# Two 256-token runs joined for their last eight steps, the first stage re-ordered, and scores put beside the v_m w_in blocks

## The chip, the cores and the metric

One Trainium2 chip, one of its cores. The metric is device time in microseconds (us) of one execution. The kernel before was timed three times: 733.68, 734.61 and 735.14 us, median 734.61.

## The reference

Eight batches, eight heads, 576 tokens, head size 64, 32 memory slots. All inputs are float32.

```python
a    = softmax(phi, axis=tokens)                 # (b, h, s, 32)
k_m  = einsum('bhsm,bhsd->bhmd', a, k)           # 32 memories per head
v_m  = einsum('bhsm,bhsd->bhmd', a, v)
attn = softmax(q @ k_m^T / 8, axis=-1)           # (b, h, s, 32)
x    = (attn @ v_m) with the heads side by side  # 4608 tokens x 512
out  = relu(x @ w_in)**2 @ w_out                 # 512 -> 2048 -> 512
```

## The kernel before

**Algebra.** The kernel never forms x. Since x @ w_in = attn @ (v_m w_in), it makes for each batch a product u = v_m w_in (256 rows, one per head and memory slot, by 2048 columns, in four blocks of 512 columns) and multiplies the attention weights a (256 rows by tokens) by it. Operands of the large products are split into a high and a low fp32r part, so a product is three matmuls: hi·hi, lo·hi, hi·lo.

**Steps.** A batch's tokens are cut into a run of 320 (WIDE) and one of 256 (NARROW). A step is one run with one of 16 tiles f of 128 hidden columns. `ffn1` (L583 to L624) does 6 matmuls (three products by two groups of heads) per piece into a PSUM tile `h`; ScalarE takes the relu (L602), VectorE the square (L608), and ScalarE and GpSimd split it into `g_hi`, `g_lo` (L618, L619). `ffn2` (L628) adds the tile's share to four PSUM accumulators `acc`: 12 matmuls (four tiles of outputs by three products). In the first 16 steps w_out tiles 0 to 3 aren't split yet and 4 plain fp32 matmuls are used (L633), each of which is two instructions. `ffn2` runs two steps behind `ffn1` (LEAD, L733). From batch 2 on, batches come in pairs: 16 steps of 320, 16 joined steps of 512 (256 tokens of each batch; 12 `ffn1` matmuls of 256, 12 `ffn2` matmuls of 512), and 16 steps of 320. Batches 0 and 1 have 64 steps of 320 or 256, in the twelve runs of L740; where a run stops before tile 16, `close` (L659) puts the sums aside in SBUF and adds later ones to them.

**Side work.** Each step has two half steps (L1013): `half(2k)` is called after `ffn1` of step k, `half(2k+1)` after `ffn2` of step k-2. The lists `plan` (L853), `early` and `late` (L948, L971) say by hand at which half each part of a side task is issued; a task is a generator, and each number in its tuple is where its next part goes. Each engine runs its instructions in this order, and so does SyncE's DMA queue (SP). Places in `early` and `late` count from the first half of a pair of batches (`begin`, L986), and those of `early` are negative: they lie in the pair before.

- `task_attend` (L357): scores (`by_heads`, L347: 8 products on 64x32 pieces of the array, 16 instructions, L353) into the PSUM tile `ps_m`; two VectorE transposes (L373), maximum, subtraction, exponential, sum, product, transpose back, and the split into `a_hi`, `a_lo`.
- `task_u` (L726, `make_u` L468): one block of u: `by_heads` over 512 columns into `ps_m`, a ScalarE copy `u_hi` (L478), a VectorE subtraction `u_lo` (L480). There is one `ps_m` (two banks), so attend and u take turns. `h` (pool `ps_h`) has two buffers, one bank each.
- `task_exp`, `task_mem`: softmax of phi and the memories of a batch (L283: 80 matmuls of 128x32 pieces).
- `decode_in`, `decode_out` (L491): the weights arrive as 64-bit words and are put back into floats by two ScalarE and three VectorE instructions and an addition (L518) on VectorE or GpSimd, whichever the place names. Split w_out then takes a ScalarE copy (L575) and a VectorE subtraction (L577).
- `spin` (L143): matmuls of an identity matrix with no use for the result.
- `task_stream`: a 1 MB block of decoded w_in back from device memory into the one tile `w0`, from batch 2 on.

The opening (L826 to L844) is a list of its own, `order`, over phi's softmax (e), batch 0's memories (m), four decodes (d0 to d3), the first two attends (a0, a1) and half a u block (u0). The DMAs ahead of it are in `loads` (L792).

Of the kernel before, what the change touches and what calls it, by code (L numbers as in the profile page):

```python
# [8 lines left out]
F32 = mybir.dt.float32  # L9
F32R = mybir.dt.float32r  # L10
# [14 lines left out]
def attn_moe_kernel(ctx: ExitStack, tc: tile.TileContext, qT, kv, phi, w_in, w_out, outT):  # L25
# [331 lines left out]
    def attend(b, t, q, mem, new_a):  # L357
# [14 lines left out]
        for half in range(2):  # L372
            nc.vector.transpose(flat[:, half * T:(half + 1) * T], sc[half][:, :T])  # L373
        done_ps(ps)
# [5 lines left out]
        yield  # L380
        nc.vector.tensor_tensor(out=st, in0=st, in1=mx[:, :, None].broadcast_to(st.shape), op=ALU.subtract)
# [344 lines left out]
    def task_u(b, n, n0=0, n1=FC):  # L726
        got = state[b]["u"].setdefault(n, [])
        w = w_at.pop((b, n)) if (b, n) in w_at else w_in_at[n]
        if (b, n) not in streamed:
            assert all(("in", 2 * n + i, qd) in ready for i in range(n0 // HC, n1 // HC) for qd in range(NQ))  # L730
        return make_u(b, n, state[b]["mem"], (n0, n1, w), got)

    LEAD = 2  # L733
# [7 lines left out]
        (((i // NT, i % NT),), Q4 * k0, Q4 * k1) for i, k0, k1 in (  # L741
            (0, 0, 1), (1, 0, 1), (2, 0, 1), (3, 0, 2), (2, 1, 2), (1, 1, 2), (0, 1, 3),
            (3, 2, 3), (0, 3, 4), (3, 3, 4), (1, 2, 4), (2, 2, 4),
        )
    ]
    for b in range(2, B, 2):
# [42 lines left out]
    def next_kv():  # L789
# [3 lines left out]
        (first_phi,),  # L793
        (first_kv, 0),
        (first_kv, 1),
        (task_q, 0, 0),
        (fetch_w_in, 0, 0),
# [22 lines left out]
    for fn, *args in loads[:later]:  # L820
# [11 lines left out]
        "d3": lambda: decode_in(1, 1),  # L832
# [6 lines left out]
        "e e e e e d0 m m m m a0 d1 d2 a1 d0 a0 a0 d1 d0 a0 a0 d3 d1 u0 d3 a0 a0 u0 u0 d3 d2 d2"  # L839
# [8 lines left out]
    for n in kept:  # L848
# [5 lines left out]
        ((2,), lambda: spin(1, ident, ps_acc.tile([P, 512], F32, name="acc0"))),  # L854
        ((0, 1, 2), decode_out, 0, nc.vector, True),
        ((0, 1, 1), decode_out, 1, nc.gpsimd, True),
        ((2, 2, 2), task_u, 0, 0, HC, 2 * HC),
        ((3,), lambda: spin(5, ident, ps_acc.tile([P, 512], F32, name="acc3"))),
        ((0,), fetch_w_in, 5, 1),
        ((0,), task_q, 1, 1),  # L860
        ((4, 7, 7), decode_out, 3, nc.vector, True),
        ((0, 1, 3, 4, 5, 5), lambda: start["a1"]),
        ((3, 5, 5, 6, 6, 7), task_exp, 1),
        ((33, 34, 37), task_u, 0, 1),
        ((21, 22, 22), decode_in, 3, 1, nc.vector),
        ((11, 11, 11), task_u, 1, 0),
        ((10, 10, 10, 10, 11, 11, 12), task_attend, 1, 0),
        ((6, 6, 7), decode_out, 2, nc.gpsimd, True),
        ((7,), fetch_w_in, 5, 0),
        ((8, 8, 9, 9), task_mem, 1),  # L870
        ((17, 18, 18), decode_in, 2, 1, nc.gpsimd),
        ((16,), fetch_w_in, 4, 1),
        ((21, 22, 23, 26, 27), decode_out, 4, nc.vector),
        ((14, 16, 16), decode_in, 2, 0),
        ((16, 16, 18, 18, 19, 20, 21), task_attend, 1, 1),
        ((24,), fetch_w_in, 7, 0),
        ((26, 30, 31), task_u, 1, 1),
        ((27, 28, 29, 31, 31), decode_out, 5, nc.vector),
        ((24, 28, 28, 30, 31), decode_out, 6, nc.gpsimd),
        ((6,), fetch_w_in, 4, 0),  # L880
        ((44,), fetch_w_out, 10),
        ((30, 31, 31, 34, 37), decode_out, 7, nc.vector),
        ((36, 37, 37), decode_in, 5, 0),
        ((31, 32, 32), decode_in, 4, 0, nc.gpsimd),
        ((43, 44, 44), decode_in, 5, 1, nc.vector),
        ((17, 22, 22), decode_in, 3, 0, nc.vector),
        ((40, 40, 40), decode_in, 4, 1, nc.vector),
        ((57,), fetch_w_out, 11),
        ((21,), fetch_w_in, 6, 1),
        ((25,), fetch_w_in, 7, 1),  # L890
        ((30,), fetch_w_out, 8),
        ((41,), fetch_w_out, 9),
        ((28,), fetch_w_in, 6, 0),
# [30 lines left out]
        ((112,), task_stream, 2, 2),  # L924
        ((94,), task_stream, 2, 0),
        ((100, 101, 102, 104, 105, 106, 112), task_attend, 2, 0),
        ((125,), task_stream, 2, 3),
        ((122, 122, 122), task_u, 2, 2),
        ((108, 109, 113, 115, 116, 117, 119), task_attend, 2, 1),
        ((101,), task_q, 2, 1),  # L930
        ((111, 112, 117), task_u, 2, 1),
        ((101, 102, 103), task_u, 2, 0),
        ((104,), task_stream, 2, 1),
        ((103,), task_phi, 3),
        ((129, 130, 130), task_u, 2, 3),
        ((99,), task_kv, 3, 0),
        ((105,), task_kv, 3, 1),
        ((120, 121, 121, 123, 124, 127), task_exp, 3),
        ((98,), u_slots.give, 5),
    ]  # L940

    for places, fn, *args in plan:
# [22 lines left out]
        ((4, 5, 6), task_u, 0, 3),  # L965
# [7 lines left out]
        ((4, 5, 7, 9), task_mem, 1),  # L973
        ((6,), task_stream, 1, 0),
# [11 lines left out]
    begin = 2 * PER * 2  # L986
# [47 lines left out]
    for k, step in enumerate(steps):  # L1034
# [62 lines left out]
```

## Time and profile before

| | |
|---|---|
| median of three runs | 734.61 us |
| the profiled execution | 734.57 us, its span 732.8 us |
| TensorE (PE) matmul busy | 716.7 us, 98% |
| VectorE (DVE) busy | 397.7 us, 54% |
| ScalarE (ACT) busy | 324.1 us, 44% |
| GpSimd (POOL) busy | 238.7 us, 33% |
| the chain that ended last | PE 82%, DVE 10%, DMA 4%, ACT 2% |

The span is what the profiler saw between the first and the last instruction; 1.8 us of the execution lie around it. PE's busy time counts an instruction from start to modelled end, and neighbours overlap, so how long a matmul really holds the engine is read from the distance of starts. The chain of waits gives that distance: its pieces follow one another without gaps.

### The profile page before, as it was taken

Reading aid. Unit: us, or ns where it says so; the run is one execution under the profiler, and the core shown is the slowest. Engines: PE = TensorE matmul, PEld = TensorE weight load, DVE = VectorE, ACT = ScalarE, POOL = GpSimd, SP = SyncE. Lnnn points to the kernel's source line nnn. Section 1 sums busy time; section 2 is a strip of 40 time slices with the busy share of each in tenths; the row PEclk is TensorE's granted clock in tenths of the full one; section 3 lists DMA queues with packets and bytes.
Section 4 is the critical chain, followed back from the end, with each engine's and each line's share of the span. In section 5 each row is a group of like instructions: output and inputs, shape, how many; then the busy total and the mean of one; then the engine's idle time right before and its main releaser. Section 6 shows DMA issues by size and latency. Waiting matters only on the chain.

```text
span 732.8 us, 14012 instructions
## 1 busy us (share of the span) xinstructions
PE 716.7 (98%) x5480; PEld 622.7 (85%) x5480; DVE 397.7 (54%) x801; ACT 324.1 (44%) x624; POOL 238.7 (33%) x275
## 2 busy tenths in 40 slices
PE   8799999999999999999999999999999999999998
PEld 4377798898889998888889899888899898888997
DVE  4988879996766626533472624733564542512211
ACT  2547866664543433423345333422444344333332
POOL 1222143442342432323333233323332242423332
PEclk9999999999999999999999999999999999999999
DMA  9991426136753911181331921154321312100101
GB/s 303 343 403 65 144 87 184 70 105 194 235 166 112 287 59 37 59 241 44 115 114 69 262 85 60 58 171 114 116 87 58 129 60 94 58 1 0 58 1 37
DMA packets 62802, 89.51 MB, mean 122 GB/s; under 512 B 3792, under 2 KB 51792, under 8 KB 59152
## 3 DMA queue, kind: packets, MB, share of 16 engines
q1 hardware_dynamic: 61936, 87.52, 36.9%
q10 hardware_dynamic: 800, 1.10, 0.5%
q8 instruction: 43, 0.70, 0.4%
q14 instruction: 23, 0.19, 0.1%
HBM read 74.97 MB, written 13.63 MB: 121 GB/s over the span
## 4 chain that ended last, share of the span: by engine, by line
PE 82%; DVE 10%; DMA 4%; ACT 2%; issue 1%; SPq 0%; POOL 0%; ACTq 0%; DVEq 0%; POOLq 0%
PE acc L641 47%; PE h L594 25%; PE ps_m L353 5%; PE acc L633 3%; PE h L283 2%; DMA w<-w_f 1%; DMA u_hi<-in_kv 1%; DVE tmp L511 1%; DVE tmp L506 1%; DVE wo L577 1%; DVE tmp L508 1%; DVE g_room L608 1%; DMA wo<-in_w_in 1%; DMA low<-in_kv 1%; DVE u_lo L480 1%
## 5 line engine op out<-in xcount | busy, mean ns | idle before, releaser
L608 DVE TENSOR_TENSOR g_room<-h,r_room 128x320 f32<-128x320 f32 (+2 forms) x192 | 101.6, 531 | 277.1 <-ACT r_room L602 262.5
L602 ACT ACTIVATE r_room<-h 128x320 f32<-128x320 f32 (+2 forms) x208 | 96.8, 465 | 273.4 <-PE h L594 266.4
L619 POOL TENSOR_TENSOR g_lo<-g_room,g_hi 128x320 fp32r<-128x320 f32 (+1 forms) x144 | 127.1, 885 | 264.3 <-DVE g_room L608 211.8
L641 PE MATMUL acc<-g_hi,wo 128*128 128x320 f32 (+1 forms) x1152 | 196.4, 307 | 0.6 <-DVE wo L577 0.6
L641 PEld LDWEIGHTS acc<-g_hi,wo 128*128 128x128 f32 x1152 | 172.0, 188 | 17.5 <-ACT r_room L602 12.6
L641 PE MATMUL acc<-o,wo 128*128 128x512 f32 x576 | 140.2, 392 | 0.0
L641 PEld LDWEIGHTS acc<-o,wo 128*128 128x128 f32 x576 | 105.2, 188 | 22.2 <-issue 1.4
L641 PE MATMUL acc<-g_lo,wo 128*128 128x320 f32 (+1 forms) x576 | 112.3, 304 | 0.0
L619 POOL TENSOR_TENSOR o<-g_room,o 128x512 fp32r<-128x512 f32 x48 | 63.0, 1312 | 145.1 <-PE acc L641 122.2
L594 PE MATMUL h<-a_hi,u_hi 128*128 128x320 f32 (+1 forms) x448 | 100.5, 306 | 1.6 <-DVE g_room L608 0.9
L594 PE MATMUL h<-a_hi,u_lo 128*128 128x320 f32 (+1 forms) x448 | 96.4, 297 | 3.2 <-DVE u_lo L480 3.2
L594 PE MATMUL h<-a_lo,u_hi 128*128 128x320 f32 (+1 forms) x448 | 96.1, 296 | 0.1
L641 PEld LDWEIGHTS acc<-g_lo,wo 128*128 128x128 f32 x576 | 90.7, 188 | 0.0
L594 PEld LDWEIGHTS h<-a_hi,u_hi 128*128 128x128 f32 x448 | 74.7, 189 | 16.3 <-issue 5.7
L594 PEld LDWEIGHTS h<-a_hi,u_lo 128*128 128x128 f32 x448 | 72.0, 189 | 4.5 <-DVE u_lo L480 4.5
L618 ACT ACTIVATE g_hi<-r_room 128x320 fp32r<-128x320 f32 (+1 forms) x144 | 67.0, 465 | 13.3 <-ACT r_room L602 1.5
L594 PEld LDWEIGHTS h<-a_lo,u_hi 128*128 128x128 f32 x448 | 72.2, 189 | 0.4 <-POOL a_lo L398 0.4
L618 ACT ACTIVATE o<-r_room 128x512 fp32r<-128x512 f32 x48 | 30.3, 632 | 56.2 <-PE acc L641 56.1
L353 PE MATMUL ps_m<-w,mem 64*32 64x512 f32 (+1 forms) x528 | 36.6, 588 | 2.0 <-POOL w L518 1.8
L480 DVE TENSOR_TENSOR u_lo<-ps_m,u_hi 128x1024 fp32r<-128x1024 f32 (+1 forms) x29 | 34.0, 1174 | 1.1 <-ACT u_hi L478 0.9
L633 PE MATMUL acc<-g_hi,wo 128*128 128x256 f32 (+1 forms) x128 | 34.1, 409 | 0.0
L633 PEld LDWEIGHTS acc<-g_hi,wo 128*128 128x128 f32 x128 | 23.2, 190 | 7.0 <-issue 1.1
(165 smaller groups left out, 646.5 us busy)
## 6 DMA issues: line engine op xcount, KB each, us to landing
w<-w_f SPq DMA_DIRECT2D x24, 1024.0 KB, 4.9
wo<-in_w_in SPq DMA_DIRECT2D x16, 512.0 KB, 8.4
wo<-in_w_out SPq DMA_DIRECT2D x16, 512.0 KB, 6.7
kvb<-in_kv SPq DMA_DIRECT2D x28, 256.0 KB, 6.8
q_sb<-in_q SPq DMA_DIRECT2D x16, 320.0 KB, 5.7
out_t<-o SPq DMA_DIRECT2D x30, 160.0 KB, 1.9
tmp<-in_kv SPq DMA_DIRECT2D x18, 256.0 KB, 5.8
e_sb<-in_phi SPq DMA_DIRECT2D x8, 512.0 KB, 7.0
```

The source lines that it names most:

```text
L283: nc.tensor.matmul(acc[M * j:M * (j + 1), col:col + w], e[c][:n, qd * P + M * j:qd * P + M * (j + 1)], y[:, j, :], start=(c == 0), stop=(c ...
L353: nc.tensor.matmul(out[half][M * pr:M * (pr + 1), :y.shape[-1]], mem[hs, x, pr], y, start=True, stop=True)
L480: nc.vector.tensor_tensor(out=u_lo[:, :, n0:n1], in0=ps[:, :, :n1 - n0], in1=u_hi[:, :, n0:n1].bitcast(F32), op=ALU.subtract)
L506: nc.vector.tensor_scalar(out=size, in0=size, scalar1=LEAST, scalar2=MOST, op0=ALU.max, op1=ALU.min)
L508: nc.vector.tensor_scalar(out=c, in0=c, scalar1=3, scalar2=0x3FFFFFF8, op0=ALU.logical_shift_left, op1=ALU.bitwise_and)
L594: nc.tensor.matmul(h[:, at:at + n], u[:, qd, fs], x[:, qd], start=(i == 0), stop=(i == len(todo) - 1))
L602: nc.scalar.activation(r, h[:, :T], AF.Relu)
L608: nc.vector.tensor_tensor(out=g, in0=h[:, :T], in1=r, op=ALU.mult)
L618: nc.scalar.activation(g_hi, r, AF.Square)
L619: nc.gpsimd.tensor_tensor(out=g_lo, in0=g, in1=g_hi.bitcast(F32), op=ALU.subtract)
L633: nc.tensor.matmul(acc[e][:, :T], wo[f][:, e * P:(e + 1) * P], g_hi, start=first, stop=last)
L641: nc.tensor.matmul(acc[e][:, :T], wo[f][:, w, e * P:(e + 1) * P], x, start=first and x is g_hi and w == 0, stop=last and x is g_lo,)
```

## The change

Five edits go together.

1. **Joined run.** Runs (0,1) and (1,1) (256 tokens each) are joined for tiles 8 to 15: eight steps of 512 in place of sixteen of 256. Batches 0 and 1 now take 56 steps, not 64, and ten runs, not twelve. The joined run's `g_hi`, `g_lo` lie in `w0`; `close` adds the two earlier partial sums.
2. **Scores beside u.** `task_both` issues the scores of an attend and one block of u in the same half step, scores first; the block's `u_hi` copy and `u_lo` go with the attend's next two parts. The scores then go into the two `h` buffers, not into `ps_m`, and the two transposes are issued right behind. It is used 11 times: once for batch 2, twice for batch 3, and four times for each of the two later pairs of batches.
3. **Opening.** Another order of `loads` and of `order`; d3's addition moves from GpSimd to VectorE.
4. **Plan.** Other places for most side tasks of the first 56 steps, and another engine for some of the additions.
5. **Spins.** In the plan, two spins are left of six (one each at halves 0 and 4; before, one at 2 and five at 3).

```diff
-    def attend(b, t, q, mem, new_a):
+    def attend(b, t, q, mem, new_a, u=None):
...
-        ps = new_ps()
-        sc = [bank(ps, half) for half in range(2)]
+        if u:
+            sc = [ps_h.tile([P, 512], F32, name="h") for _ in range(2)]
+        else:
+            ps = new_ps()
+            sc = [bank(ps, half) for half in range(2)]
         by_heads(sc, mem, 0, q)
+        if u:
+            next(u)
+            for half in range(2):
+                nc.vector.transpose(flat[:, half * T:(half + 1) * T], sc[half][:, :T])
         yield
...
+        if u:
+            next(u)
+        else:
+            for half in range(2):
+                nc.vector.transpose(flat[:, half * T:(half + 1) * T], sc[half][:, :T])
+            done_ps(ps)
...
+        if u:
+            next(u, None)
...
+    def task_both(b, t, n):
...
+        return attend(b, t, state[b]["q"].pop(t), state[b]["mem"], new, task_u(b, n))
...
     runs = [
-            (0, 0, 1), (1, 0, 1), (2, 0, 1), (3, 0, 2), (2, 1, 2), (1, 1, 2), (0, 1, 3),
-            (3, 2, 3), (0, 3, 4), (3, 3, 4), (1, 2, 4), (2, 2, 4),
+            ((0,), 0, 1), ((1,), 0, 1), ((2,), 0, 1),
+            ((3,), 0, 2), ((2,), 1, 2), ((1,), 1, 2),
+            ((0,), 1, 3), ((1, 3), 2, 4), ((0,), 3, 4),
+            ((2,), 2, 4),
...
     loads = [
         (first_phi,),
+        (first_kv, 1),
         (first_kv, 0),
-        (first_kv, 1),
-        (task_q, 0, 0),
         (fetch_w_in, 0, 0),
+        (task_q, 0, 0),
...
+        (next_kv,),
+        (fetch_w_out, 1),
         (fetch_w_out, 0),
-        (fetch_w_out, 1),
-        (next_kv,),
...
-        "e e e e e d0 m m m m a0 d1 d2 a1 d0 a0 a0 d1 d0 a0 a0 d3 d1 u0 d3 a0 a0 u0 u0 d3 d2 d2"
+        "e e e e e d0 m m m m a0 d0 d1 d2 a0 a0 a1 d1 d0 a0 d3 d1 u0 a0 d3 u0 a0 u0 d2 d3 d2 a0"
...
     plan = [
...
-        ((26, 30, 31), task_u, 1, 1),
+        ((25, 29, 29), task_u, 1, 1),
-        ((82, 85, 85, 88, 89), decode_out, 15, nc.vector),
+        ((78, 80, 80, 82, 82), decode_out, 15, nc.vector),
-        ((88,), task_kv, 2, 1),
+        ((84,), task_kv, 2, 1),
-        ((92, 93, 93, 93), task_mem, 2),
+        ((86, 86, 87, 87), task_mem, 2),
-        ((94,), task_stream, 2, 0),
+        ((91,), task_stream, 2, 0),
-        ((101, 102, 103), task_u, 2, 0),
-        ((108, 109, 113, 115, 116, 117, 119), task_attend, 2, 1),
+        ((101, 102, 103, 104, 105, 106, 107), task_both, 2, 1, 0),
-        ((111, 112, 117), task_u, 2, 1),
+        ((107, 108, 109), task_u, 2, 1),
...
-        ((-28, -27, -26), task_u, 0, 0),
-        ((-36, -35, -34, -33, -32, -31, -30), task_attend, 0, 0),
+        ((-35, -34, -33, -32, -31, -30, -29), task_both, 0, 0, 0),
-        ((-20, -19, -18), task_u, 0, 1),
-        ((-23, -22, -21, -20, -19, -18, -17), task_attend, 0, 1),
+        ((-23, -22, -21, -20, -19, -18, -17), task_both, 0, 1, 1),
...
-        ((14, 15, 16), task_u, 1, 0),
-        ((10, 11, 12, 13, 14, 15, 16), task_attend, 1, 0),
+        ((13, 14, 15, 16, 17, 18, 19), task_both, 1, 0, 0),
-        ((26, 27, 28), task_u, 1, 1),
-        ((35, 36, 37, 38, 39, 40, 41), task_attend, 1, 1),
+        ((27, 28, 29, 30, 31, 32, 33), task_both, 1, 1, 1),
```

## Rows read from the trace of the kernel before

**Rows 1.** The page, busy time by engine, and the granted clock.
```profile
PE 716.7 (98%) x5480; PEld 622.7 (85%) x5480; DVE 397.7 (54%) x801; ACT 324.1 (44%) x624; POOL 238.7 (33%) x275
...
PEclk9999999999999999999999999999999999999999
```

**Rows 2.** Stretches of 10 us: busy PE, PEld, DVE, ACT, POOL, clock, DMA share, GB/s.
```profile
80.00:90.00 10.00, 8.81 (x56) 6.49 (x41) 8.39 (x14) 8.41 (x18) 1.27 (x1) 1.00 0.67 236
...
130.00:140.00 10.00, 9.33 (x64) 9.06 (x62) 9.73 (x16) 7.04 (x15) 3.64 (x4) 1.00 0.16 52
...
160.00:170.00 10.00, 9.72 (x67) 9.04 (x66) 9.55 (x22) 6.13 (x13) 4.58 (x5) 1.00 0.20 52
170.00:180.00 10.00, 8.42 (x125) 7.61 (x124) 5.20 (x12) 3.01 (x7) 3.80 (x10) 1.00 0.72 223
```

**Rows 3.** Chain of waits, 405 to 460 us: start, length, what.
```profile
406.72 1.76 PE acc L641 x12
...
412.01 0.92 PE ps_m L353 x16
412.94 1.96 PE acc L641 x12
...
418.42 1.02 PE ps_m L353 x16
419.44 1.96 PE acc L641 x12
...
452.44 2.75 PE acc L641 x12
455.19 1.43 PE h L594 x12
```

**Rows 4.** Chain of waits, first stage: a step of 256 tokens, a u block.
```profile
96.54 1.42 PE acc L641 x12
97.96 0.71 PE h L594 x6
...
143.18 1.94 PE ps_m L353 x16
```

**Rows 5.** Chain of waits: scores of 320 and of 256 tokens between steps.
```profile
280.61 0.70 PE ps_m L353 x16
281.31 1.63 PE h L594 x12
...
362.07 0.59 PE ps_m L353 x16
```

**Rows 6.** Timeline of PE, 17 to 18 us: two blocks of scores side by side.
```profile
17.12 0.50 PE L353 MATMUL acc<-q_sb,mem 64*32 64x320 f32 x7
...
17.92 0.40 PE L353 MATMUL acc<-a_lo,mem 64*32 64x256 f32 x4
```

**Rows 7.** Timeline of DVE, 406 to 424 us: transposes of scores, and a square.
```profile
413.01 0.78 DVE L373 STREAM_TRANSPOSE st<-ps_m 128x256 f32<-128x256 f32 x2
...
419.00 0.49 DVE L608 TENSOR_TENSOR g_room<-h,r_room 128x320 f32<-128x320 f32 x1 [1.56 <-ACT r_room L602]
```

**Rows 8.** Who PE waited for: us in total, times, longest.
```profile
PE h L594 <- DVE u_lo L480: 3.2, 3, 1.5
...
PE ps_m L283 <- DMA low<-in_kv: 1.1, 1, 1.1
```

**Rows 9.** Chain of waits: the load of a w_in block for batch 2.
```profile
193.36 8.52 DMA w<-w_f
```

**Rows 10.** Groups of PE by form: the spins after the opening.
```profile
L148 PE MATMUL acc<-ident 128*128 128x512 f32 x14 | 6.6, 599 | 0.0
```

**Rows 11.** Chain of waits: the second half of the first u block.
```profile
38.70 0.60 DVE u_lo L480
```

**Rows 12.** Groups of DVE by form: u_lo, and an addition of a decode.
```profile
L480 DVE TENSOR_TENSOR u_lo<-ps_m,u_hi 128x1024 fp32r<-128x1024 f32 x27 | 32.7, 1211 | 1.1 <-ACT u_hi L478 0.9
...
L518 DVE CUSTOM_DVE_ANT_0 w<-tmp,low 128x1024 uint16<-128x1024 uint16 x7 | 4.8, 692 | 0.5
```

More of the change, by code (lines that the diff above doesn't have):

```diff
@@ L371, in attend @@
             return
-        for half in range(2):
-            nc.vector.transpose(flat[:, half * T:(half + 1) * T], sc[half][:, :T])
-        done_ps(ps)
+        if u:
[4 more added lines that the diff above has]
+            done_ps(ps)
         mx = one.tile([P, nblk], F32, name="mx")
@@ L665, in close @@
             return
+        if len(pieces) > 1 and pieces[:1] in aside:
+            got = [aside.pop((piece,)) for piece in pieces]
+            for e in range(NET):
+                x0 = 0
+                for (b, t), (o, _, _) in zip(pieces, got):
+                    x1, at = x0 + width(b, t), b * S + tokens(b, t)[0]
+                    nc.vector.tensor_tensor(out=o[e], in0=acc[e][:, x0:x1], in1=o[e], op=ALU.add)
+                    nc.sync.dma_start(out=outT[e * P:(e + 1) * P, at:at + x1 - x0], in_=o[e])
+                    x0 = x1
+            for _, slots, taken in got:
+                for i in taken:
+                    slots.give(i)
+            return
         if pieces in aside:
@@ L705, in task_mem @@
         kvs = kvs or state[b]["kv"]
+        assert len(kvs) == NQ
         new_mem(b)
@@ L731, in task_u, with new @@
         return make_u(b, n, state[b]["mem"], (n0, n1, w), got)
+    def task_both(b, t, n):
+        def new():
+            state[b]["a"][t] = new_a(width(b, t))
+            return state[b]["a"][t]
+        return attend(b, t, state[b]["q"].pop(t), state[b]["mem"], new, task_u(b, n))
     LEAD = 2
@@ L740, in attn_moe_kernel @@
     runs = [
-        (((i // NT, i % NT),), Q4 * k0, Q4 * k1) for i, k0, k1 in (
-            (0, 0, 1), (1, 0, 1), (2, 0, 1), (3, 0, 2), (2, 1, 2), (1, 1, 2), (0, 1, 3),
-            (3, 2, 3), (0, 3, 4), (3, 3, 4), (1, 2, 4), (2, 2, 4),
+        (tuple((i // NT, i % NT) for i in p), Q4 * k0, Q4 * k1) for p, k0, k1 in (
[4 rows of a table added]
         )
     ]
+    FIRST = sum(f1 - f0 for _, f0, f1 in runs)
     for b in range(2, B, 2):
@@ L853, in attn_moe_kernel @@
     plan = [
[L854 to L862, printed above, removed]
+        ((4,), lambda: spin(1, ident, ps_acc.tile([P, 512], F32, name="acc3"))),
@@ L863, in attn_moe_kernel @@
+        ((2, 2, 3), task_u, 0, 0, HC, 2 * HC),
+        ((1, 2, 2), decode_out, 0, nc.vector, True),
+        ((6, 6, 7), decode_out, 2, nc.vector, True),
+        ((0,), lambda: spin(1, ident, ps_acc.tile([P, 512], F32, name="acc0"))),
+        ((1,), task_q, 1, 1),
+        ((1, 4, 4), decode_out, 1, nc.gpsimd, True),
+        ((3, 8, 8), decode_out, 3, nc.vector, True),
+        ((2,), fetch_w_in, 5, 1),
         ((3, 5, 5, 6, 6, 7), task_exp, 1),
-        ((33, 34, 37), task_u, 0, 1),
+        ((0, 3, 3, 4, 5, 5), lambda: start["a1"]),
@@ L865, in attn_moe_kernel @@
+        ((14,), fetch_w_in, 6, 1),
         ((21, 22, 22), decode_in, 3, 1, nc.vector),
+        ((13,), fetch_w_in, 4, 0),
+        ((10, 10, 10, 10, 11, 11, 12), task_attend, 1, 0),
         ((11, 11, 11), task_u, 1, 0),
-        ((10, 10, 10, 10, 11, 11, 12), task_attend, 1, 0),
-        ((6, 6, 7), decode_out, 2, nc.gpsimd, True),
-        ((7,), fetch_w_in, 5, 0),
+        ((11,), fetch_w_in, 5, 0),
         ((8, 8, 9, 9), task_mem, 1),
-        ((17, 18, 18), decode_in, 2, 1, nc.gpsimd),
@@ L872, in attn_moe_kernel @@
-        ((16,), fetch_w_in, 4, 1),
-        ((21, 22, 23, 26, 27), decode_out, 4, nc.vector),
-        ((14, 16, 16), decode_in, 2, 0),
+        ((17, 18, 19), decode_in, 2, 1, nc.gpsimd),
+        ((15,), fetch_w_in, 4, 1),
+        ((14, 16, 16), decode_in, 2, 0, nc.gpsimd),
         ((16, 16, 18, 18, 19, 20, 21), task_attend, 1, 1),
-        ((24,), fetch_w_in, 7, 0),
-        ((26, 30, 31), task_u, 1, 1),
-        ((27, 28, 29, 31, 31), decode_out, 5, nc.vector),
-        ((24, 28, 28, 30, 31), decode_out, 6, nc.gpsimd),
@@ L880, in attn_moe_kernel @@
[L880 to L885, printed above, removed]
+        ((23,), fetch_w_in, 7, 0),
+        ((25, 29, 29), task_u, 1, 1),
+        ((25, 29, 30, 32, 32), decode_out, 5, nc.vector),
+        ((44, 44, 44), decode_in, 5, 1, nc.gpsimd),
+        ((45,), fetch_w_out, 10),
+        ((24, 28, 28, 30, 31), decode_out, 6, nc.gpsimd),
@@ L886, in attn_moe_kernel @@
+        ((27,), fetch_w_in, 6, 0),
+        ((32, 33, 34, 36, 39), decode_out, 7, nc.vector),
+        ((29,), fetch_w_out, 8),
+        ((36, 37, 38), decode_in, 5, 0, nc.gpsimd),
+        ((32, 34, 37), task_u, 0, 1),
+        ((31, 32, 32), decode_in, 4, 0, nc.vector),
         ((17, 22, 22), decode_in, 3, 0, nc.vector),
-        ((40, 40, 40), decode_in, 4, 1, nc.vector),
+        ((40, 40, 40), decode_in, 4, 1, nc.gpsimd),
         ((57,), fetch_w_out, 11),
-        ((21,), fetch_w_in, 6, 1),
@@ L890, in attn_moe_kernel @@
[L890 to L893, printed above, removed]
+        ((20, 23, 24, 26, 27), decode_out, 4, nc.vector),
+        ((22,), fetch_w_in, 7, 1),
+        ((37,), fetch_w_out, 9),
+        ((50, 51, 54, 54, 55), decode_out, 10, nc.vector),
         ((50, 51, 52), task_u, 0, 2),
+        ((53, 54, 54, 55, 58), decode_out, 9, nc.vector),
+        ((58,), fetch_w_out, 12),
+        ((64, 67, 67), decode_in, 7, 1, nc.vector),
@@ L930, in attn_moe_kernel @@
-        ((101,), task_q, 2, 1),
-        ((111, 112, 117), task_u, 2, 1),
-        ((101, 102, 103), task_u, 2, 0),
[L933 to L939, printed above, removed]
+        ((58, 59, 61, 64, 65), decode_out, 11, nc.vector),
+        ((60, 61, 63), decode_in, 6, 0, nc.vector),
@@ new lines, in attn_moe_kernel @@
+        ((46, 47, 47, 50, 51), decode_out, 8, nc.gpsimd),
+        ((68,), fetch_w_out, 15),
+        ((75,), fetch_w_out, 13),
+        ((67, 69, 70, 73, 74), decode_out, 12, nc.gpsimd),
+        ((74,), fetch_w_out, 14),
+        ((71, 71, 72), task_u, 0, 3),
+        ((63, 65, 65), decode_in, 6, 1, nc.vector),
+        ((64, 65, 67), decode_in, 7, 0, nc.gpsimd),
+        ((56,), task_phi, 2),
+        ((76, 76, 76, 79, 79), decode_out, 13, nc.vector),
+        ((77, 78, 78, 79, 82), decode_out, 14, nc.gpsimd),
@@ new lines, in attn_moe_kernel @@
+        ((89, 89), split_out, 2),
+        ((53,), task_kv, 2, 0),
+        ((84,), task_q, 2, 0),
+        ((80, 82), split_out, 0),
+        ((75, 77, 79, 80, 80, 82), task_exp, 2),
+        ((86, 86), split_out, 3),
+        ((75, 75, 76), task_u, 1, 3),
+        ((84,), task_kv, 2, 1),
+        ((78, 80, 80, 82, 82), decode_out, 15, nc.vector),
+        ((86, 86, 87, 87), task_mem, 2),
+        ((91,), task_stream, 2, 0),
+        ((102,), task_stream, 2, 1),
+        ((88, 88, 89, 91, 91, 94, 96), task_attend, 2, 0),
@@ L940, in attn_moe_kernel @@
+        ((89, 89), split_out, 1),
+        ((112,), task_stream, 2, 3),
+        ((101, 102, 103, 104, 105, 106, 107), task_both, 2, 1, 0),
+        ((107, 108, 109), task_u, 2, 1),
+        ((85,), task_q, 2, 1),
+        ((107,), task_stream, 2, 2),
+        ((90,), task_phi, 3),
+        ((89,), task_kv, 3, 0),
+        ((91,), task_kv, 3, 1),
+        ((111, 112, 112), task_u, 2, 2),
+        ((107, 108, 108, 110, 111, 113), task_exp, 3),
+        ((87,), u_slots.give, 5),
     ]
@@ L985, in attn_moe_kernel @@
     ]
-    begin = 2 * PER * 2
+    begin = 2 * FIRST
     for n, b in enumerate(range(2, B, 2)):
@@ L1042, in attn_moe_kernel @@
         T = sum(width(*x) for x in pieces)
-        if T > WIDE and not broad:
-            rooms = [const.tile([P, 2, T], F32R, name=f"o{o_slots[NARROW].take()}") for _ in range(2)]
-            broad.extend((rooms[0][:, i], rooms[1][:, i]) for i in range(2))
+        if T > WIDE and f == runs[i][1] and (k < FIRST or len(broad) < 3):
+            if k < FIRST:
+                rooms = const.tile([P, 4, T], F32R, name="w0")
+                rooms = [rooms[:, :2], rooms[:, 2:]]
+            else:
+                rooms = [const.tile([P, 2, T], F32R, name=f"o{o_slots[NARROW].take()}") for _ in range(2)]
+                broad[:] = [None]
+            broad[:0] = [(rooms[0][:, i], rooms[1][:, i]) for i in range(2)]
         g, rest = ffn1(f, parts, T, k, "act" if k < SQ_ACT else "dve", k < WHOLE and f in whole)
```

55 lines of the change are left out of this document (14 added, 41 removed).

## The prediction

> **What bounds the kernel now.** I read the page first: PE is busy 716.7 of 732.8 us and its clock is granted in full in every slice [rows 1], so time can come only from what PE itself is given to do and from the few places where it waits. Then the stretches of 10 us: the waits lie in the first stage. PE is short of 10 us by 1.19, 0.67, 0.28 and 1.58 in four of them, 3.7 us together, and DVE is at 9.5 to 9.7 of 10 in two of these four [rows 2]. PE's list of waits names u_lo on DVE (3.2 us; two of the three are in the opening) and the load of batch 2's keys and values [rows 8]; another is hidden in a busy number, a u block of 1.94 us where 1.02 is usual [rows 3, 4]. Last the chain of waits, for what PE's work costs where nothing holds it up. A 320-token step has an ffn2 of 1.76 us for 12 matmuls, so 0.147 us each; a 256-token step 1.42 and 0.71 (0.119 each); a joined step 2.75 and 1.43 (0.229 per matmul of 512) [rows 3, 4]. A `by_heads` block between two steps takes 1.02 us for u and 0.70 or 0.59 for scores of 320 or 256, and what follows it is 0.20 longer (1.96 for 1.76, 1.63 for 1.43) [rows 3, 5]. So a block costs 1.22, 0.90 or 0.79.
>
> **The change part by part.**
>
> *Joined run.* Two steps of 256 take 2 x (1.42 + 0.71) = 4.26 us, a joined one 2.75 + 1.43 = 4.18; by the matmuls, 24 x 0.119 - 12 x 0.229 = 0.11 [rows 3, 4]. I take 0.1 on PE, 0.8 us in eight steps (0.6 to 0.9). By the Trainium skill (TensorE: Matmul & The Clock Gate, section Back-to-back issue gap) a matmul of N columns takes N/2.4 ns and 2.5 ns at full clock; halving the count would then save only 12 x 2.5 ns a step, 0.24 us in eight. The rows have 119 and 229 ns where the page's formula has 109 and 216, and they decide.
>
> *Scores beside u, 11 times.* Each block pays once for going in and once for coming out. Coming out is the 0.20. Going in I get from the three sizes: 1.02, 0.70 and 0.59 fit 0.16 and 0.00167 per column [rows 3, 5]. Whether two blocks side by side pay it once, the opening shows: there the second halves of a 320 and a whole 256 block run from 17.12 to about 18.29 [rows 6], 1.17 us, while 0.53 and 0.43 of columns and 0.16 once are 1.12. So a pair saves 0.36, less perhaps 0.05. The bounds are 0 (both still pay all) and 0.36; I take 0.33, near the measured pair, 11 x 0.33 = 3.6 us. One of the replaced attends took 0.92 where 0.59 is usual [rows 3, 5], and so did its twin in the next pair. I put that down to the memories, whose last part stands one half ahead (9 and 10); now it is four (9 and 13). That is 2 x 0.33 = 0.7 us more (0 to 0.7).
>
> What the new place adds is two waits. The second score tile takes the `h` that the step's ffn1 has just filled, so PE must have its relu and square behind it; and the next ffn1 takes the first score tile, so its transpose must be done. The square of a 320 step starts at 419.00 and ends at 419.49, 1.07 us after its ffn1 ended at 418.42 [rows 3, 7]; ffn2 lies between, 1.76 us. That is 0.7 us in hand, and more in a joined step. The two transposes take 0.78 us for 256 [rows 7], the first about half of it, while u's 0.85 us of columns run on PE. Behind a waiting PE stand the u block and the next ffn1, then ACT's relu; a wait there costs its full length. I take 0, with up to 1.3 us each as the other end: a DVE piece as long as u_lo (1.21 us [rows 12]) ahead of the square and of the transposes. Since `ps_m` is held for one block, not two, no other task waits longer for it. The streams of w_in move with their u blocks and keep seven halves or more in the pairs, as before.
>
> *Opening and spins.* Keys and values of the second group come first, the first w_in block ahead of q: the same bytes on the same saturated queues. ACT decodes d0 earlier, but the softmax that follows is a row of DVE instructions, and these, the decodes and the first two attends fill DVE up to the second half of the first u block, which ends at 39.30 [rows 11] and lets step 2 go. An addition joins them (d3 on DVE, 0.69 to 1.2 us), another (tile 1's decode) now comes behind that point. I take nothing, -2 to +2. Four spins of two instructions go, at 6.6/14 = 0.47 us each [rows 10], 3.8 us; they stood where PE waited for that u_lo, so they hid in it and give nothing back. The Trainium skill (same page, section Why this matters for your kernels) warns that PE idling between bursts falls back to half clock; the rows show a full clock with these spins in place, and none shows it without them.
>
> *Plan.* By the places, additions of decodes on DVE go from 17 to 18 (+0.7 us [rows 12]), `close` does four adds fewer, and eight squares of 512 stand for sixteen of 256. So DVE's load hardly changes; its deadlines do. The joined steps are twice as long, so tiles 12 to 15 of w_out, which are wanted in step 40 before and after, are wanted some 8 us later in DVE's time (four steps of 4.18 in place of 2.14). u(1,1) is finished at half 29, not 31, three halves ahead of its first use: that is the u_lo for which PE stands in the stretch of 80 to 90 us. Batch 2's keys and values are asked for four halves after decode_out 15 has given back its buffers, across two joined steps (8.4 us), not two steps of 256 (4.3): that is the wait of 1.1 and the 1.58 of 170 to 180. I let go 1.2 + 0.3 + 1.6 = 3.1 of the 3.7 us [rows 2, 8]. The decodes before u(0,3), behind the 0.67 of 130 to 140 and the block of 1.94, stay in their place (halves 60 to 71, the same steps of 320): nothing there.
>
> Against it: `w0` is lent to the joined run, so batch 2's first w_in block can't be loaded before step 43's ffn2, at half 91, and stands on SP behind five loads of batch 3's keys, phi and the joined run's eight stores. One such load took 8.52 us under like traffic [rows 9], and u wants it ten halves (13 us) later; some fifteen issues stand ahead of it on SP. I take 0.6 us of new waits here and at the two blocks that keep only four halves (5.3 us); 0 to 4.
>
> The sum, from the profiled execution (734.57, of which 732.8 is span; the median is 734.61, so nothing has to be shifted): -0.8 - 3.6 - 0.7 - 3.1 + 0.6 = -7.6, so 727.0 us.
>
> **The rivals.**
>
> - *The pairs save nothing* (10 in 100): blocks side by side pay their way in and out each. For it: instructions that follow a block are 0.20 longer whatever it is. Against: the opening's pair [rows 6]. 727.0 + 3.6 = 730.6.
> - *The first stage gets faster by more* (13): u(0,3) waits less too (0.9 of its 1.94 us [rows 4]), the opening comes 2 us earlier, pairs save 0.36. 722 to 723.
> - *New waits in the first stage* (13): every place but a few moved, on a DVE that is full [rows 2], and the block for batch 2 is loaded in the thick of SP's queue. 4 to 9 us of the kind in rows 8 and 9: 731 to 736, 733.5 in the middle. A lighter PE doesn't help there.
> - *The clock falls in the opening* (5): without the spins PE has little to do in the microseconds ahead of that u_lo. If it runs at 1.2 GHz for the next 4 to 8 us, the matmuls in them take twice as long, partly in DVE's shadow: +2 to +6, 729 to 733.
> - *Slower: the scores wait in `h`* (7). Place: the second score tile and the ffn1 behind, in all 11 pairs. It decides once DVE runs more than 0.7 us late at the end of ffn2. DVE is half idle in the pairs [rows 1], which speaks against it; pieces of 1.21 us [rows 12] speak for it. At 1.3 us each, 14 us: 727.0 + 14.3 = 741. It outweighs the gain from 0.7 us each on.
>
> **How the numbers follow.** The forecast itself has 50 in 100, between 724 and 730.5: pairs 0.2 to 0.36, the first stage 1 to 4 us. What a measurement here can tell from no change is 0.2%, 1.5 us, so 733.1 to 736.1 is the same. Of the new waits' 13, 4 end faster, 5 the same and 4 slower; of the clock's 5, 4 faster and 1 the same; of the remaining 2, one each. Faster: 50 + 10 + 13 + 4 + 4 = 81. Same: 5 + 1 + 1 = 7. Slower: 7 + 4 + 1 = 12. The range of 8 in 10 takes in the forecast, the pairs that save nothing, the faster first stage and most of the new waits: 720.5 to 734.5.
>
> **What would show it.** A pair of scores and u should take about 0.53 + 0.85 + 0.16 = 1.55 us in the chain with one 0.20 behind (320), and the next ffn1 should start without idle time ahead of it that a DVE transpose ended. A joined step of the first stage should show 2.75 and 1.43. PE's waits should lose the line for DMA low, and that for u_lo should shrink to what the opening has; a line for DMA w or for DVE st (the transposes) would be the new waits. Step 2's ffn1 should go on at about 39 us and the clock stay full in the first two slices. The prediction is wrong if the span falls by less than 3 us although the pairs show their saving, for then the first stage took the rest; and wrong in its main term if PE idles at the pairs.

## The result, and the profile after

The changed kernel takes 725.8 us (median of four, 725.36 to 726.19) beside 734.47 for the kernel before: 0.9883 of its time, with a 95% interval of 0.987 to 0.9897, so 8.7 us less. 727.0 had been forecast, with 720.5 to 734.5 around it. The profiled execution's span is 723.5 us, 9.3 less than before.

The two lines of the changed kernel's page that answer [rows 1]; the second is the granted clock in 40 slices.

```profile
PE 707.9 (98%) x5376; PEld 617.8 (85%) x5376; DVE 386.0 (53%) x790; ACT 321.4 (44%) x608; POOL 235.5 (33%) x266
...
PEclk9999999999999999999999999999999999999999
```

PE is as full as before and has 8.8 us less to do. The 40 slices hide one thing that stretches of 10 us show (columns as in [rows 2]): the clock fell in the opening.

```profile
30.00:40.00 10.00, 6.73 (x35) 3.99 (x34) 9.55 (x20) 6.18 (x12) 1.60 (x1) 0.83 1.10 333
...
80.00:90.00 10.00, 10.00 (x65) 7.89 (x64) 7.66 (x14) 8.72 (x20) 2.10 (x2) 1.00 0.53 203
...
130.00:140.00 10.00, 9.34 (x64) 9.08 (x63) 9.76 (x16) 5.33 (x10) 4.45 (x4) 1.00 0.16 52
...
160.00:170.00 10.00, 10.00 (x62) 8.91 (x62) 8.71 (x17) 6.05 (x11) 5.06 (x4) 1.00 0.00 0
170.00:180.00 10.00, 9.49 (x116) 7.72 (x115) 4.54 (x8) 3.43 (x6) 3.04 (x8) 1.00 0.42 120
```

PE's shortfall (what it lacks of 10 us busy) is gone from 80 to 90 and from 160 to 170 us, down from 1.58 to 0.51 from 170 to 180, and the same from 130 to 140. (Two of 0.57 and 0.79 are new, at 120 to 130 and 210 to 220 us.) Who PE waited for (answering [rows 8]):

```profile
PE h L606 <- DVE u_lo L492: 2.1, 2, 1.1
PE h L606 <- ACT u_hi L490: 1.5, 1, 1.5
...
PE ps_m L353 <- DVE u_lo L492: 0.8, 1, 0.8
PE h L606 <- DVE g_room L620: 0.7, 1, 0.7
PE acc L653 <- ACT low L516: 0.6, 1, 0.6
...
PE ps_m L283 <- DMA low<-in_kv: 0.4, 1, 0.4
```

The third u_lo is gone, and the load of batch 2's keys is down from 1.1 to 0.4 us. Two lines behind the opening are new, and they are the two new shortfalls: an ffn2 that waits for ScalarE, by the list for a decode's `low` (0.6 us, at 124 us), and a u block that waits for the u_lo ahead of it (0.8 us, at 218 us). The wait for u_hi stands in the opening, at 33 to 35 us, where it was 0.5 us in two pieces. The pairs in the chain of waits (start, length, what):

```profile
242.17 0.59 PE h L353 x16
242.76 0.86 PE ps_m L353 x16
243.62 1.07 PE h L606 x6
...
262.33 0.70 PE h L353 x16
263.03 0.86 PE ps_m L353 x16
263.89 1.08 PE h L606 x6
```

Scores of 256 and a u block cost 0.59 + 0.86 + 0.19 = 1.64 us where they had cost 0.79 + 1.22 = 2.01 apart [rows 3, 5]: u doesn't pay its own way in (0.86, not 1.02), and the two share one way out (0.19). No piece of DVE's stands between a pair and the ffn1 behind it.

Where the time went, by places that both kernels have. Batch 1's scores, the end of the opening, in the kernel before, in the changed one and in e7 (below), which has the old opening:

```profile
54.55 0.85 PE ps_m L353 x16
```

```profile
53.33 0.85 PE ps_m L353 x16
```

```profile
53.65 0.85 PE ps_m L353 x16
```

Step 2's ffn1 gets its u_lo 3.0 us earlier (36.31 for 39.35), but batch 1's scores are only 1.2 earlier. Behind u(1,1) the lead is 2.9 (ffn2 at 91.15 for 94.10), before u(0,3) 2.4 (140.80 for 143.18), and at the first joined ffn1 of batches 2 and 3 it is 4.85 (269.37 for 274.22). There the changed kernel has done one more block: the second scores of batch 3, which cost the kernel before 0.90 us behind that place [rows 5]. With them the lead is 5.75, and the 3.55 that are left to the span's 9.3 are what eight more pairs and the memories' wait of two attends make (8 x 0.36 + 2 x 0.33 = 3.54).

### The profile page after: what moved, and what is told of

Same layout as the page of the kernel before. It is cut to its first block, busy times and chain, and to the rows that moved or that the text cites. A ratio compares the mean times of both kernels' runs of the same rounds, so it can differ in the third digit from the quotient of the medians.

```text
span 723.5 us, 13722 instructions
## 1 busy us (share of the span) xinstructions
PE 707.9 (98%) x5376; PEld 617.8 (85%) x5376; DVE 386.0 (53%) x790; ACT 321.4 (44%) x608; POOL 235.5 (33%) x266
## 4 chain that ended last, share of the span: by engine, by line
PE 86%; DVE 8%; DMA 3%; ACT 1%; issue 1%; POOL 1%; SPq 0%; ACTq 0%; DVEq 0%; POOLq 0%
PE acc L653 48%; PE h L606 26%; PE ps_m L353 4%; PE acc L645 4%; PE h L283 2%; DMA u_lo<-in_kv 1%; PE h L353 1%; DVE tmp L523 1%; DMA e_sb<-in_phi 1%; DVE tmp L520 1%; DVE tmp L518 1%; DVE g_room L620 1%; DMA low<-in_kv 1%; DVE wo L589 1%; DVE u_lo L492 0%
## 5 line engine op out<-in xcount | busy, mean ns | idle before, releaser
L631 POOL TENSOR_TENSOR g_lo<-g_room,g_hi 128x320 fp32r<-128x320 f32 (+1 forms) x128 | 113.8, 891 | 239.9 <-DVE g_room L620 224.9
L653 PE MATMUL acc<-g_hi,wo 128*128 128x320 f32 (+1 forms) x1024 | 175.5, 308 | 0.6 <-ACT low L516 0.6
L653 PEld LDWEIGHTS acc<-g_hi,wo 128*128 128x128 f32 x1024 | 155.7, 188 | 6.7 <-ACT r_room L614 1.7
L653 PE MATMUL acc<-g_lo,wo 128*128 128x320 f32 (+1 forms) x512 | 100.7, 307 | 0.0
L653 PEld LDWEIGHTS acc<-g_lo,wo 128*128 128x128 f32 x512 | 81.5, 188 | 0.0
L630 ACT ACTIVATE g_hi<-r_room 128x320 fp32r<-128x320 f32 (+1 forms) x128 | 60.3, 471 | 10.9 <-ACT r_room L614 0.4
L353 PE MATMUL ps_m<-w,mem 64*32 64x512 f32 (+1 forms) x528 | 36.3, 584 | 3.0 <-POOL w L530 2.2
L490 ACT CAST u_hi<-ps_m 128x1024 fp32r<-128x1024 f32 (+1 forms) x29 | 28.3, 975 | 9.2 <-PE ps_m L353 8.9
```

What stands on the lines that cost most here:

```text
L353: nc.tensor.matmul(out[half][M * pr:M * (pr + 1), :y.shape[-1]], mem[hs, x, pr], y, start=True, stop=True)
L490: nc.scalar.copy(u_hi[:, :, n0:n1], ps[:, :, :n1 - n0])
L630: nc.scalar.activation(g_hi, r, AF.Square)
L631: nc.gpsimd.tensor_tensor(out=g_lo, in0=g, in1=g_hi.bitcast(F32), op=ALU.subtract)
L653: nc.tensor.matmul(acc[e][:, :T], wo[f][:, w, e * P:(e + 1) * P], x, start=first and x is g_hi and w == 0, stop=last and x is g_lo,)
```

## The experiments

Each was timed beside the kernel before, in five rounds, e8 in three. Ratios are to that kernel, with 95% intervals; 0.001 is 0.73 us. The changed kernel's own is 0.9883 (0.987 to 0.9897). "So much above the changed kernel" is the difference of two such ratios, unless medians are named; most have 1 us of uncertainty or more.

**e1, the pairs apart again; e2, the pairs alone.** e1 takes ten of the eleven out of the changed kernel, e2 puts the same ten into the kernel before.

```diff
-        ((13, 14, 15, 16, 17, 18, 19), task_both, 1, 0, 0),
+        ((14, 15, 16), task_u, 1, 0),
+        ((10, 11, 12, 13, 14, 15, 16), task_attend, 1, 0),
...
```

> The changed kernel with ten of its eleven pairs taken apart again: scores and u blocks of batches 3 to 7 at the places of the kernel before (the pair in batch 2 stays). Theory (a pair saves one way in and one way out, 0.36 us, and the attends at half 13 no longer wait for the memories, 2 x 0.33): 10 x 0.36 + 0.66 = 4.3 us slower than the changed kernel, about 730.1. Rival (blocks side by side pay as much as apart, the gain is the first stage's): 0 to 0.7 us slower, 726 to 726.5.

> The kernel before with the ten pairs of batches 3 to 7 alone (first 64 steps as they were, except that u(2,3) comes three halves later). Theory: 4.3 us faster than before, about 730.2. Rival (pairs save nothing): 734.5. A third (the pairs save only where the first stage leaves DVE free, so that parts don't add up): another number than the difference of the changed kernel and the kernel with its pairs apart.

e1: 0.9946 (0.9934 to 0.9958), 731.02 us, 0.0063 or 4.6 us above the changed kernel. e2: 0.9942 (0.9929 to 0.9955), 730.37 us, 4.3 us below the kernel before. The theory's 4.3 from both sides: the pairs are half of the gain, and they add up with the rest. The memories' wait is seen too: the scores of 256 at half 10 in e1, and at half 13 beside u in the changed kernel:

```profile
408.44 0.92 PE ps_m L353 x16
```

```profile
409.93 0.59 PE h L353 x16
```

**e8, the pairs one half earlier.**

```diff
-        ((13, 14, 15, 16, 17, 18, 19), task_both, 1, 0, 0),
+        ((12, 14, 15, 16, 17, 18, 19), task_both, 1, 0, 0),
...
```

> The changed kernel with the ten pairs of batches 3 to 7 one half earlier, between ffn1 and ffn2 of a step in place of behind ffn2. Theory (the second score tile takes the h that ffn1 has just filled, and relu and square end 1.07 us after it): PE waits about 1 us in every pair, 10 us in all, about 736, slower than the kernel before. Rival (the tile of scores comes free as soon as relu has read it, or PE has other work): 0 to 5 us slower.

738.05 us, 1.0048 (1.0034 to 1.0063): 12 us above the changed kernel and slower than the kernel before. The chain of e8 at one of the ten, in a step of 320:

```profile
260.71 0.90 PE h L606 x6
...
261.63 0.45 ACT r_room L614
...
262.17 0.50 DVE g_room L620
...
262.72 0.50 PE h L353 x7
```

From ffn1's end at 261.61 PE stands until 262.72, through relu and square: 1.1 us, and so at eight of the ten. The other two lie in joined steps, whose relu and square have 512 columns:

```profile
332.93 1.44 PE h L606 x12
...
335.89 0.50 PE h L353 x7
```

That is 1.5 us, from 334.37. Together they are 11.9 of the 12 us. So the wait that was forecast as the slower rival exists; what hides it is the ffn2 between, 1.76 us in a step of 320.

**e3, the joined run apart in four pieces; e11, in three.** All later places move with it. A run end is where `close` puts the sums aside.

```diff
-            ((0,), 1, 3), ((1, 3), 2, 4), ((0,), 3, 4),
+            ((0,), 1, 3), ((1,), 2, 3), ((3,), 2, 3), ((1,), 3, 4), ((3,), 3, 4), ((0,), 3, 4),
```

```diff
+            ((0,), 1, 3), ((1,), 2, 3), ((3,), 2, 4), ((1,), 3, 4), ((0,), 3, 4),
```

> The changed kernel with its joined run cut into sixteen steps of 256 (four tiles of one run, four of the other, twice), all later places moved so that every task keeps its time and every tile its deadline. Theory (the joined run saves matmuls alone, 0.1 us a step): 0.9 us slower than the changed kernel, 726.7. Rival (it is the joined steps that free the first stage of its waits, by fewer squares, relus and sums on DVE and ACT): 2 to 4 us slower, 728 to 730.

> The kernel with the joined run apart once more, but with one run end less: four tiles of (0,1), eight of (1,1), four of (0,1). Theory (beside its matmuls the joined run is worth the run ends it saves, each a set of sums on a full DVE that the next run's accumulators wait for): 0.8 to 1.5 us faster than with four pieces, 728.0 to 728.8. Rival (what counts is squares and relus of 256 in place of 512, all through): the same as with four pieces, 729.6.

e3: 0.9933 (0.9921 to 0.9946), 729.58 us, 3.7 us above the changed kernel, where the matmuls account for 0.9. e11, with one run end less: 0.9898 (0.988 to 0.9916), 727.55 us, 1.1 us above the changed kernel by the ratios, 1.8 by the medians. e3 fits its rival's 2 to 4 us, not the theory, and e11 lies 2.6 us below it (2.0 by the medians), more than its theory's 0.8 to 1.5, though with intervals of 1 us and more each; *the same as with four pieces* is out. PE's waits of e3 have a line that the changed kernel's lack and that is 0.2 us in e11, the accumulators waiting for `close` on DVE:

```profile
PE acc L653 <- DVE o L694: 1.5, 2, 1.3
```

So in e3 the run ends on a full DVE cost PE 1.5 us in this wait; what the rest of the difference is, and how much the moved places do, was not taken apart. The kernel before had as many run ends there as e11 (five from step 36 on), so against it the joined run is worth some 1.1 to 1.8 us, of which 0.9 are matmuls; the intervals would allow the matmuls alone.

**e5, u(1,1) late again; e12, u(1,1) early alone.** e12 makes the same move in the kernel before.

```diff
-        ((25, 29, 29), task_u, 1, 1),
+        ((26, 30, 31), task_u, 1, 1),
```

> The changed kernel with u(1,1) back at halves 26, 30 and 31. Theory (u_lo behind the decodes of half 30 and 31 was the wait of 1.2 to 1.6 us at 88 us): 1 to 1.6 us slower, 726.8 to 727.4. Rival (DVE is full later on, so a wait here only moves): 0 to 0.4 us slower.

> The kernel before with u(1,1) alone moved, from halves 26, 30 and 31 to 25, 29 and 29. Theory (its u_lo stood behind two decodes on DVE, 1.0 us of PE's wait and the u_hi copy before it; the stages behind have room to keep the gain): 1.2 to 1.8 us faster than before. Rival (in the kernel before DVE is full from 110 to 170 us, so what is won at 88 us is waited for there): 0 to 0.5 us faster.

e5: 0.9908 (0.9894 to 0.9922), 728.2 us, 1.8 us above the changed kernel; the wait is back in its chain, a u_lo (89.57, 1.15 us) ahead of an ffn1 at 90.76. Its profiled execution comes out of the opening 1.9 us late (batch 1's scores at 55.26); behind u(1,1) it is 4.0 late, and it still is before u(0,3) (144.81 for 140.80) and at the end (3.9). So here the move costs 2.1 us, and neither delay is made up later. e12: 0.9991 (0.9975 to 1.0007), 733.87 us, no difference that can be told. e12's chain says where the gain went. Its u(0,3) still starts 1.7 us earlier than before (141.48 for 143.18); then, and below it the same pieces of the kernel before:

```profile
170.64 5.11 DMA low<-in_kv
175.88 0.43 PE ps_m L283 x8
...
192.76 8.79 DMA w<-w_f
201.69 1.09 PE ps_m L353 x16
```

```profile
172.28 4.46 DMA low<-in_kv
...
176.87 0.43 PE ps_m L283 x8
...
202.02 1.09 PE ps_m L353 x16
```

The load of batch 2's keys starts 1.6 us earlier but takes 0.65 longer, and its w_in block takes 8.79 us, not 8.52 [rows 9]; the lead is 1.0 us behind the first and 0.3 behind the second. The rival was right that the gain is waited away, and wrong about where. In the changed kernel PE waits 0.4 us for the keys and has no line for the w_in block, and u(1,1)'s gain stays (e5).

**e4, spins for the clock.**

```diff
-        ((4,), lambda: spin(1, ident, ps_acc.tile([P, 512], F32, name="acc3"))),
+        ((3,), lambda: spin(3, ident, ps_acc.tile([P, 512], F32, name="acc3"))),
```

> The changed kernel with three spins at half 3 in place of the one at half 4: PE is busy while it waits for the second half of the first u block. Theory (the clock fell to 1.2 GHz at 36 us because PE had little to do from 31 to 36 us; what it cost is partly in the shadow of the row of DVE work up to 42 us): clock 1.00 all through, and 0.5 to 1 us faster than the changed kernel, about 725.0. Rival 1 (the low clock lay on the path with its whole 1.9 us): 1.9 to 2.7 us faster. Rival 2 (hidden by DVE, or given back later): no difference.

0.9887 (0.9875 to 0.99), 726.29 us: no difference. The clock stays full in e4; in the changed kernel it was at its lower level, 1.2 GHz, from about 36.4 to 39.8 us (worked out from stretches of 1 us); in the two stretches from 34 to 36 us PE had been busy for 0.32 and 0.23 us. Three of these stretches, then one of 10 us of e4:

```profile
35.00:36.00 1.00, 0.23 (x2) 0.00 (x0) 1.00 (x3) 0.31 (x1) 0.00 (x0) 1.00 1.04 336
36.00:37.00 1.00, 0.69 (x3) 0.69 (x4) 0.97 (x3) 0.32 (x1) 0.00 (x0) 0.70 0.98 375
37.00:38.00 1.00, 1.00 (x4) 0.82 (x4) 0.93 (x4) 0.00 (x0) 0.00 (x0) 0.50 1.07 374
```

```profile
30.00:40.00 10.00, 9.23 (x52) 5.70 (x51) 9.51 (x20) 5.83 (x12) 1.60 (x1) 1.00 1.11 323
```

DVE is full either way, and what PE gains at 40 us in e4 it waits for DVE at batch 1's softmax of phi:

```profile
PE ps_m L180 <- DVE nmx L175: 1.9, 1, 1.9
```

From step 2's go-ahead (u_lo's end) batch 1's scores are 16.7 us away in e4 and in e7, whose clock is full there, 17.1 in the changed kernel, and 17.8 in the profiled executions of e1, e5 and e11, whose clock stays low to between 41.5 and 42.5 us. So in the traces the fall goes with 0.4 to 1.1 us, which e4's times don't show.

**e7, the old opening.** `loads` and `order` of the kernel before, and d3's addition on GpSimd.

```diff
-        "e e e e e d0 m m m m a0 d0 d1 d2 a0 a0 a1 d1 d0 a0 d3 d1 u0 a0 d3 u0 a0 u0 d2 d3 d2 a0"
+        "e e e e e d0 m m m m a0 d1 d2 a1 d0 a0 a0 d1 d0 a0 a0 d3 d1 u0 d3 a0 a0 u0 u0 d3 d2 d2"
...
```

> The changed kernel with the opening of the kernel before: its loads, its order, and d3's addition on GpSimd again. Theory (the opening's gain is what is left of it when batch 1's scores go, 1.2 us): 1 to 1.5 us slower, about 727. Rival 1 (it is worth the whole 3.0 us by which step 2 goes earlier): 3 us slower. Rival 2 (nothing: step 2's gain comes from the plan, which no longer decodes w_out tile 1 ahead of that u block): within 0.5 us.

0.9881 (0.9869 to 0.9894), 725.96 us. The theory falls, rival 2 holds: the new opening alone changes nothing. Nor does it make the opening's lead: with the old one step 2's ffn1 gets its u_lo at 37.03, 2.3 us earlier than in the kernel before, and batch 1's scores go at 53.65, 0.9 earlier. What e7 keeps of the change there are the plan, with tile 1's decode behind that u block, and the spins.

**e6 and e9, batch 3's softmax of phi elsewhere.** The u block that waits 0.8 us at 218 us stands behind a u_lo which stands behind this softmax on DVE. e6 moves the softmax ahead; e9 moves u(2,1)'s last two parts ahead of it.

```diff
-        ((107, 108, 108, 110, 111, 113), task_exp, 3),
+        ((96, 97, 97, 98, 98, 100), task_exp, 3),
```

```diff
-        ((107, 108, 109), task_u, 2, 1),
+        ((107, 107, 108), task_u, 2, 1),
-        ((107, 108, 108, 110, 111, 113), task_exp, 3),
+        ((108, 109, 109, 111, 112, 113), task_exp, 3),
```

> The changed kernel with batch 3's softmax of phi at halves 96 to 100 in place of 107 to 113, where DVE has room. Theory (in the changed kernel u_lo of u(2,1) stands behind it on DVE, holds ps_m, and the next u block waits 0.8 us): 0.8 us faster, about 725.0. Rival (a new wait in its place: phi's load not there yet, or the transposes of the pair at half 101 late): 0 to 2 us slower.

> The changed kernel with u(2,1)'s u_hi copy at half 107 and its u_lo at 108, and batch 3's softmax of phi behind them, at 108 to 113. Theory (u_lo stood behind that softmax on DVE and held ps_m, 0.8 us of PE's time; no run ends there, so nothing else waits for DVE): 0.8 us faster than the changed kernel, about 725. Rival (the softmax now ends later and batch 3's memories wait for it, at half 116): no difference, or up to 1 us slower.

e6: 0.997 (0.9959 to 0.9981), 732.56 us, 6.4 us above the changed kernel, outside both expectations. A run ends at half 98, and its sums (L694) now wait on DVE behind the softmax; PE waits 5.1 us for the accumulators, its clock falls (0.74 granted in these 10 us), and the next ffn2 takes 3.54 us in place of 1.76. PE's list, the chain, and the stretch:

```profile
PE acc L653 <- DVE o L694: 5.1, 1, 5.1
```

```profile
203.17 1.94 DVE e_sb L227 x5
205.11 0.41 DVE o L694
205.52 0.14 issue
205.66 3.54 PE acc L653 x12
```

```profile
200.00:210.00 10.00, 4.86 (x35) 3.88 (x41) 6.80 (x21) 2.27 (x4) 1.73 (x2) 0.74 0.56 162
```

e9: 724.86 us (724.62 to 725.3), 0.9862 (0.9841 to 0.9883). The line for the waiting u block is gone from its list. The ratios' intervals overlap, but its four times lie below the changed kernel's four (725.36 to 726.19) and those of e10 beside it on the same chip (725.67 to 727.32): about 1 us faster, and the fastest version here.

**e10, an addition moved off DVE.**

```diff
-        ((58, 59, 61, 64, 65), decode_out, 11, nc.vector),
+        ((58, 59, 61, 64, 65), decode_out, 11, nc.gpsimd),
```

> The changed kernel with the addition of w_out tile 11's decode on GpSimd in place of VectorE. Theory (DVE is what PE waits for at 120 to 140 us, so an addition less on it shortens the wait): 0.4 to 0.7 us faster. Rival (VectorE's own decode instructions run at half speed beside a GpSimd addition, 1.0 in place of 0.44 us, and tile 11 and the g_lo behind it come later): 0 to 1 us slower.

0.988 (0.9861 to 0.9899), 725.97 us: no difference, the lower end of the rival's 0 to 1 us. PE's wait for the square there is 1.1 us, not 0.7. The trace bears out the rival's mechanism. The addition on GpSimd and the decode instruction beside it on DVE in e10, then the addition and the same instruction, both on DVE, in the changed kernel's chain:

```profile
128.69 1.30 POOL L530 TENSOR_TENSOR tmp<-tmp,low 128x512 int32<-128x512 int32 x1
```

```profile
128.73 1.54 DVE L518 TENSOR_SCALAR tmp<-tmp 128x512 f32<-128x512 f32 x1
```

```profile
128.56 0.60 DVE tmp L530
129.16 0.35 DVE tmp L518
```

In e10 the two overlap and DVE's ends 0.28 us behind GpSimd's; from the u_lo ahead of it to its end DVE takes 1.5 us where it had taken 0.95 with the addition on DVE.

## Why the prediction was right, point by point

- **Pairs: 3.6 + 0.7 forecast for eleven.** e1 and e2 give 4.6 and 4.3 for ten of them with the memories' wait, where ten at the forecast 0.33 and the wait make 4.0. The reading of way in and way out from three sizes was right to 0.03 us: a pair saves the whole 0.36. *The pairs save nothing* is out.
- **No wait in `h`: right, and shown by e8.** The 1.07 us from ffn1's end to the square's end were read from one row of a step of 320; e8 pays 1.1 us in such steps and 1.5 in joined ones, where ffn2 isn't between.
- **Joined run: 0.8 forecast, 1.1 to 1.8 measured** (e11). The matmuls were counted right. That two run ends go was left out; in e3 the run ends cost PE 1.5 us in its wait for `close`, but e11's interval is too wide to say that the term was too small. The formula that the prediction quotes from the Trainium skill (TensorE: Matmul & The Clock Gate, section Back-to-back issue gap) is given there for an isolated matmul; the sum went by the rows.
- **First stage: 3.1 less 0.6 forecast.** For u(1,1) 1.2 was forecast and e5 has 1.8. What was left of batch 2's keys is 0.4 of 1.1 us. That the gain at u(1,1) depends on what these loads leave of it (e12) the prediction didn't see; it added them as if each stood alone. The block before u(0,3) waits as before (1.93 us for 1.94), as forecast. New waits: 0.6 us at 124 us, from ScalarE, and 0.8 us at u(2,2), from the DVE queue; the load of w_in, which had been suspected, left no line.
- **Opening and spins: nothing forecast, and that was the term that was off.** e7 and e4 time no difference for the new order and for the spins. But tile 1's decode, which the plan moves, is in both, and with it batch 1's scores come 1.2 us earlier in the changed kernel's profiled execution and 0.9 in e7's. Step 2 was to go on at 39 us and went at 36.3, and the clock was to stay full and fell. The prediction had set d3's addition, which joins DVE's row, equal to tile 1's decode, which leaves it. The first took 0.69 us, the second's three instructions 1.6, and two pieces of the row ran shorter (a_lo 0.80 for 1.87, an addition 0.69 for 1.68). The rival's price for the clock, 2 to 6 us, was too high: the fall lay mostly in DVE's shadow (0.4 to 1.1 us in the traces, nothing that e4 could time). The lead is from single executions, and those with the changed opening reach batch 1's scores anywhere from 53.1 to 55.3 us; no run takes tile 1's decode alone back.
- **The sum.** By the leads of the two profiled executions: the opening 1.2 (0 forecast), the first stage behind it 2.6 (2.5), the joined run's matmuls 0.9 (0.8), eleven pairs with the memories' wait 4.6 (4.3); together the span's 9.3 (the medians differ by 8.7). The 2.6 are what the other three leave: u(1,1)'s 1.7, less 0.6 for the new wait at 124 us, and 1.4 between u(0,3) and the joined steps, which also hold the joined run's two run ends; these 1.4 were not tried one by one. So the sum came out near for its reasons. It was low mainly by the opening's term, which had been set to nothing without a row for it.

## What to carry to other kernels

Put small blocks of the same tiling side by side: here each excursion from 128-wide to 64x32 matmuls and back cost 0.36 us of a full PE, with blocks of 256, 320 and 512 columns alike. When a block borrows a buffer that the main loop has just filled, put the longest stretch of independent work in between; the same edit half a step earlier turned a gain of 4.6 us over the pairs apart (e1) into a loss of 7.5. A wait taken away early is only worth what the next load leaves of it: 0.3 of 1.7 us in e12, all of it in the changed kernel, where PE hardly waits for the loads. Look for that load before adding up.

## What was not expected of the hardware

Two pieces of VectorE's work in the opening took less than half as long in the changed kernel: the two a_lo subtractions 0.80 us for 1.87 (at 27.8 us in both), and an addition of a decode 0.69 for 1.68. In the kernel before a GpSimd addition ran beside each of them, in the changed one GpSimd stood still. The a_lo of the kernel before, of the changed kernel, and of e7, where d3's addition is on GpSimd again (27.46 to 28.84 us):

```profile
27.81 1.87 DVE a_lo L439 x2
```

```profile
27.77 0.80 DVE a_lo L451 x2
```

```profile
27.32 1.87 DVE a_lo L451 x2
```

e7 changes the order and the loads too. e10 moves one addition alone, and there a DVE instruction of 0.42 us takes 1.54 beside it. So the neighbour is the cause in e10 and the likely one in the opening. Not every DVE instruction pays: in the changed kernel a square of 320 takes 0.48 us with GpSimd at g_lo (131.60 us; g_lo from 131.26 to 133.72) and with GpSimd idle (126.94).
